# Transposes and mask product in 32-column tiles, and the two parts of an attend back to back, in a recurrent-memory transformer kernel

## The chip, the cores and the metric

The kernel runs on one core of a Trainium2 chip. The metric is the device time of one execution in microseconds (us), the median over runs. Ratios are the mean time of one kernel's fast runs over that of the other's of the same rounds on the same chip, so they are not quite the ratio of the medians that are quoted beside them. A ratio is given with its 95% interval. Profiles are of single executions, and fast runs of one kernel lie up to 15 us (the kernel before) apart, so a difference of some 15 us between two profiles is not clear by itself.

## The reference

Two branches are mixed by a gate. Branch A is a transformer layer with a recurrent memory: 64 segments of 32 tokens, each with 8 memory rows that the segment before it has written. Branch B is a GEGLU feed-forward layer, which does not depend on A.

```python
def _A_ref(x, mem0, Wq, Wk, Wv, Wo, seg_len):        # Dm = 1024, 32 heads of 128, M = 8, seg_len = 32
    mem = mem0
    for s in range(n_seg):                           # 64 segments, each needs mem of the one before
        h = jnp.concatenate([mem, xs], axis=1)       # 40 rows
        q, k, v = (einsum of h with Wq, Wk, Wv)      # cut
        scores = jnp.where(mask, q @ k.T * scale, -1e9)
        o = softmax(scores) @ v
        o = jnp.einsum('bhte,hed->btd', o, Wo)
        mem = o[:, :M, :].copy()
        outs.append(o[:, M:, :])
g = sigmoid((x * gate_w).sum(-1, keepdims=True))
return g * a + (1 - g) * b                           # b = (gelu(x @ w_gate) * (x @ w_up)) @ w_down
```

## The kernel before

The kernel has three parts: a first one of some 100 us that prepares x and a share of the feed-forward layer, the 64 segments (about 25 us each), and the rest of the feed-forward layer from about 1,700 us on. The change touches the segments alone. The kernel does not keep all weights of the attention (four times 8 MB) in SBUF, the on-chip memory: most of each segment's weights are loaded again, by loads of 512 KB into slots.

In a segment the 32 rows of h are the stationary operand of most matmuls, the one that a weight load puts into the array. They fill 32 columns of the array (128*32 in the profile, where the full form is 128*128), so four matmuls run side by side (in the trace they start 3 to 4 ns apart), each in one quarter of the columns and each writing 32 partitions of PSUM, where results are collected. From there a copy evacuates them to SBUF. Three kinds of work leave this tiling: the transposes of the evacuated q and k and the mask product (stationary operand of 128 columns), and the attend (32 rows).

```python
def trans4(e, t=tok):                                     # about five times per segment
    for j in range(4):
        ins = e.transpose(PBV[TT][:, j * 128:(j + 1) * 128], t[:, j * 128:(j + 1) * 128], ident[:, :])
    return ins

def scores(r, mid=None):
    def f(e):
        e.matmul(PB[SS][:, 0:320]..., lhsT=ident[:, :], rhs=mS..., start=True, stop=False)   # the mask, by the array
        for lo, hi, c in ((0, 32, 0), (32, 40, 40)):
            for j in range(4):
                for g in range(4):                        # 32 small matmuls, 32-column tiles
                    ins = e.matmul(PB[SS][32 * g:32 * g + hi - lo, ...], lhsT=qT or qkr, rhs=kT[:, j, g, :], ...)
    ...                                                   # softmax on VectorE and ScalarE: cut

def attend(u):       # 16 matmuls, 32 rows each, into four banks: lhsT=vA[r, j, :], rhs=tA[r, ...]
def attend_tail(u):  # 4 more for the remaining 8 keys: lhsT=vB[r, u, :], rhs=tB[r, ...]; then oT is copied

def proj(p, s):      # one of 64 steps of a segment, 512 KB of weights
    ...              # q, k, v:
                for g in range(4):
                    ins = e.matmul(PB[bk][32 * g:32 * g + 32, :], lhsT=h[:, i, :], rhs=w[:, g * 512:(g + 1) * 512], ...)
    ...              # o:
                for hh in range(2):
                    for g in range(4):
                        c = hh * 1024 + g * 256
                        ins = e.matmul(PB[XO][32 * g:32 * g + 32, 0:256], lhsT=oT[:, gp_, 2 * jj + hh, 0:32], rhs=w[:, c:c + 256], ...)
```

Between the steps stand "fills" (`some(f1, 2)` issues two steps of them), which project the carried rows of later segments. Each segment ends with the carry: the output bank is evacuated, transposed and copied into the next segment's h.

## Time and profile before

| | kernel before |
|---|---|
| median of 3 runs | 2232.4 us (2222.9 to 2234.9) |
| span of the profiled run (an execution of its own) | 2236.0 us |
| 60 segments (third carry to last of 63) | 1479 us, 24.7 us each |
| PE instructions (matmuls and weight loads) | 73,284; 334 more of PE's sequencer |

These are lines of the page of the kernel before. "PE" counts matmuls and "PEld" weight loads; in the 40-slice rows a digit is a tenth; q8 is the queue that brings instructions: packets, MB, share of the engines' time.

```profile
PE 2082.7 (93%) x36642; PEld 1097.3 (49%) x36642; DVE 905.4 (40%) x2152; ACT 611.3 (27%) x1296; POOL 616.0 (28%) x1139
...
PEclk9989999999999999999999999999999999999999
DMA  9977887788788778878887788788779410000000
...
q8 instruction: 287, 4.70, 0.8%
```

PE is busy nearly all the time, and DMA is at 70 to 80% through the segments. The 287 packets are of 16,384 bytes, and 73,284 / 256 = 286 (with the sequencer's instructions 287.6): one packet for 256 PE instructions. Such 256 instructions are called a block here, and the step from one to the next a boundary.

PE's list of waits in the kernel before (line, waited for: us in total, times, longest us). L770 is the output projection, L758 the projections, L992 the carry transposes, L800 a fill.

```profile
PE pb L770 <- issue: 40.2, 38, 2.4
PE pb L992 <- ACT a_bf L658: 12.9, 34, 0.4
PE pb L758 <- issue: 10.0, 10, 1.7
PE pb L758 <- DMA sl<-in_A_Wv_dram: 7.1, 11, 0.9
PE pb L770 <- DMA sl<-in_A_Wo_dram: 5.9, 9, 1.1
PE pb L800 <- issue: 5.3, 8, 1.3
```

"issue" means that PE waited for nothing the profile can name. In the start times of the PE instructions of the segments, counted through with the sequencer's, 54 gaps of over 0.7 us stand at one and the same position of every 256, and no other position has more than two. At each of them the next block's packet had started 2.2 to 2.6 us earlier in nearly every case. So these are waits for instructions. Each of the 70 issue waits of the segments ends within 0.25 us of a boundary, of which there are 247. In the segments the packet of a block starts from 0.7 us before to 5.5 us after the first instruction of the block before it runs, 2.5 us after it in the median.

The timeline of PE in a segment of the kernel before, where two visits to the full tiling can be seen (start, duration, line, tile as rows*columns, count):

```profile
911.88 1.91 PE L758 MATMUL pb<-sl,hT 128*32 128x512 bf16 x32
913.72 0.40 PE L670 MATMUL pb<-ident,tok 128*128 128x128 bf16 x4
914.05 0.83 PE L758 MATMUL pb<-sl,hT 128*32 128x512 bf16 x12
914.81 0.31 PE L685 MATMUL pb<-mS,ident 128*128 128x320 bf16 x1
915.05 0.28 PE L691 MATMUL pb<-kT,qT 128*32 128x40 bf16 x16
```

The start of the first transpose to the start of the next projection is 914.05 - 913.72 = 0.33 us, and the first transpose itself starts 312 ns after the last projection, where a projection would have started after 216 ns. This extra time at a change of tiling, on the way in and on the way out, is called a drain below; the name is no more than that, as the trace does not show what the array does in it. By differences of start times it is 96 to 106 ns on the way in (312 less the 216 or 206 ns from one group of projection matmuls to the next) and 93 to 105 ns on the way out (from the last transpose to a projection 149 ns, less the 56 ns from transpose to transpose; from the mask to the scores 240 ns, less 135).

### The profile page before, as it was taken

To read this page: it belongs to the slowest core of one execution; us is meant where nothing else is said; L and a number is where in the kernel's file an instruction comes from. 1 tells how busy PE (TensorE), PEld (TensorE's weight loads), DVE (VectorE), ACT (ScalarE), POOL (GpSimd) and SP (SyncE) were. 2 spreads that over 40 slices of the span, in tenths; PEclk is the share of its full clock that TensorE was granted. 3 is DMA by queue.
4 is the path that set the end of the run, shared out by engine and by line. 5 is a ranking of instruction groups with operands and counts; after the bars stand their busy time and mean duration, and the time that the engine had idled before them with its cause. 6 is when DMAs were issued, how large, how long until landed. Compare 5 with 4: busy or idle time off the path is not lost.

```text
span 2236.0 us, 80061 instructions
## 1 busy us (share of the span) xinstructions
PE 2082.7 (93%) x36642; PEld 1097.3 (49%) x36642; DVE 905.4 (40%) x2152; ACT 611.3 (27%) x1296; POOL 616.0 (28%) x1139
## 2 busy tenths in 40 slices
PE   7889999999899899999999899999888999999999
PEld 4334555455555555555554555555444444444444
DVE  5433343343344333433443344334334516354362
ACT  4322232223232232322223232223222303122130
POOL 5133334332433343233333323343321000000000
PEclk9989999999999999999999999999999999999999
DMA  9977887788788778878887788788779410000000
GB/s 319 406 274 278 296 305 266 277 309 285 265 303 307 262 266 297 295 280 283 287 293 276 267 304 294 270 284 316 277 268 356 179 38 29 29 24 33 19 29 19
DMA packets 203440, 529.04 MB, mean 237 GB/s; under 512 B 29592, under 2 KB 46616, under 8 KB 203104
## 3 DMA queue, kind: packets, MB, share of 16 engines
q1 hardware_dynamic: 174064, 471.93, 58.9%
q0 software_dynamic: 28896, 51.75, 7.3%
q8 instruction: 287, 4.70, 0.8%
q10 hardware_dynamic: 144, 0.26, 0.1%
q14 instruction: 49, 0.40, 0.0%
HBM read 490.16 MB, written 33.55 MB: 234 GB/s over the span
## 4 chain that ended last, share of the span: by engine, by line
PE 77%; DMA 11%; issue 4%; POOL 4%; DVE 1%; ACT 1%; SPq 1%; DVEq 0%; POOLq 0%; ACTq 0%
PE pb L758 25%; PE pb L446 15%; PE pb L770 9%; PE pb L1098 8%; PE pb L785 7%; PE pb L670 4%; DMA sl<-in_A_Wo_dram 3%; PE pb L800 3%; DMA sl<-in_A_Wv_dram 3%; DMA a_scr<-a_bf 2%; PE pb L691 2%; PE pb L685 1%; POOL v_scr L826 1%; PE pb L1080 1%; PE pb L724 1%
## 5 line engine op out<-in xcount | busy, mean ns | idle before, releaser
L758 PE MATMUL pb<-sl,hT 128*32 128x512 bf16 x12288 | 749.5, 382 | 24.7 <-issue 10.0
L758 PEld LDWEIGHTS pb<-sl,hT 128*32 128x32 bf16 x12288 | 331.2, 97 | 292.1 <-issue 19.9
L770 PE MATMUL pb<-sl,oT 128*32 128x256 bf16 x8192 | 283.1, 276 | 48.9 <-issue 40.2
L658 ACT ACTIVATE tok<-pb 128x512 bf16<-128x512 f32 x317 | 189.3, 597 | 408.6 <-PE pb L758 368.3
L743 POOL COPY oRc<-oT 128x128 bf16<-128x128 bf16 x128 | 96.8, 757 | 645.9 <-DVE oT L661 627.5
L770 PEld LDWEIGHTS pb<-sl,oT 128*32 128x32 bf16 x8192 | 207.7, 97 | 100.8 <-issue 52.9
L785 PE MATMUL pb<-sl,hR 128*32 128x512 bf16 x3072 | 226.6, 385 | 11.3 <-DMA sl<-in_A_Wq_dram 5.1
L446 PE MATMUL pb<-xT,wg 128*128 128x512 bf16 x768 | 182.6, 381 | 2.9 <-DMA wg<-in_B_w_gate_dram 2.9
L446 PE MATMUL pb<-xT,wu 128*128 128x512 bf16 x768 | 182.0, 380 | 0.0
L1098 PE MATMUL pb<-wd,GT 128*128 128x512 bf16 x784 | 169.9, 379 | 0.0
L661 DVE CAST oT<-pb 128x160 bf16<-128x160 f32 x256 | 71.2, 320 | 211.0 <-PE pb L734 210.7
L658 ACT ACTIVATE vA<-pb 128x512 bf16<-128x512 f32 x128 | 76.4, 597 | 267.2 <-PE pb L758 267.2
L434 ACT ACTIVATE s<-pb 128x512 f32<-128x512 f32 x112 | 66.9, 597 | 295.1 <-PE pb L446 295.1
L661 DVE COPY kT<-pb 128x512 bf16<-128x512 bf16 x128 | 51.9, 406 | 228.0 <-PE pb L670 93.7
L670 PE MATMUL pb<-ident,tok 128*128 128x128 bf16 x1268 | 126.7, 222 | 5.5 <-DVE kT L661 2.2
L670 PEld LDWEIGHTS pb<-ident,tok 128*128 128x128 bf16 x1268 | 72.2, 98 | 113.7 <-ACT tok L658 86.0
L435 DVE SCALAR_TENSOR_TENSOR tp<-s,pb 128x512 f32<-128x512 f32 x112 | 76.8, 686 | 125.6 <-ACT s L434 125.3
L1098 PEld LDWEIGHTS pb<-wd,GT 128*128 128x128 bf16 x784 | 76.7, 98 | 92.5
L446 PEld LDWEIGHTS pb<-xT,wg 128*128 128x128 bf16 x768 | 75.2, 98 | 94.2 <-issue 4.6
L696 DVE TENSOR_REDUCE st<-pb 128x8 f32<-128x320 f32 x128 | 63.0, 492 | 142.7 <-PE pb L691 142.6
L446 PEld LDWEIGHTS pb<-xT,wu 128*128 128x128 bf16 x768 | 75.4, 98 | 91.3 <-issue 1.3
L1045 POOL DMA_DIRECT2D out_dram<-osb x14 | 7.6, 545 | 372.5 <-PE pb L446 224.6
(96 smaller groups left out, 2149.3 us busy)
## 6 DMA issues: line engine op xcount, KB each, us to landing
sl<-in_A_Wv_dram SPq DMA_DIRECT2D x394, 512.0 KB, 8.9
sl<-in_A_Wo_dram SPq DMA_DIRECT2D x205, 512.0 KB, 6.1
sl<-in_A_Wk_dram SPq DMA_DIRECT2D x142, 512.0 KB, 5.5
sl<-in_A_Wq_dram SPq DMA_DIRECT2D x79, 512.0 KB, 7.0
qkr<-qk_scr POOLq DMA_DIRECT2D x126, 64.0 KB, 2.2
qk_scr<-stg POOLq DMA_DIRECT2D x61, 128.0 KB, 6.0
wd<-in_B_w_down_dram SPq DMA_DIRECT2D x7, 1024.0 KB, 14.7
px<-in_A_x_dram SPq DMA_DIRECT2D x16, 256.0 KB, 6.7
```

What stands on the lines that cost most here:

```text
L434: op("act", lambda e: e.activation(s1[:, :], hg, ACTF.Square, scale=SQ), rd=[BK(bg)], wr=[s1.r()])
L435: op("dve", lambda e: e.scalar_tensor_tensor(out=t[:, :], in0=s1[:, :], scalar=1.0, in1=hg, op0=ALU.add, op1=ALU.mult), rd=[BK(bg), s1.r() ...
L446: ins = e.matmul(PB[bk][:, 0:FB], lhsT=w[:, kc, cc:cc + 128], rhs=x[:, :, :, kc, :].rearrange("p t i c -> p (t i) c"), start=(kc == 0), st ...
L658: op("act", lambda e: e.activation(o, i, ACTF.Copy), rd=rd, wr=wr)
L661: op("dve", lambda e: e.tensor_copy(o, i), rd=rd, wr=wr)
L670: ins = e.transpose(PBV[TT][:, j * 128:(j + 1) * 128], t[:, j * 128:(j + 1) * 128], ident[:, :])
L743: op("pool", lambda e: e.tensor_copy(oRc[:, u, :, :].rearrange("p c x -> p x c"), oT[:, :, :, 32:40].rearrange("p g j c -> p (g j) c")), r ...
L758: ins = e.matmul(PB[bk][32 * g:32 * g + 32, :], lhsT=h[:, i, :], rhs=w[:, g * 512:(g + 1) * 512], start=(p % 8 == 0), stop=(p % 8 == 7))
L770: ins = e.matmul(PB[XO][32 * g:32 * g + 32, 0:256], lhsT=oT[:, gp_, 2 * jj + hh, 0:32], rhs=w[:, c:c + 256], start=(r == 0 and p % 8 == 0 ...
L785: ins = e.matmul(PB[b][32 * g:32 * g + 32, :], lhsT=h[:, k[2], :], rhs=w[:, g * 512:(g + 1) * 512], start=(n == 0), stop=(n == 7))
L800: ins = e.matmul(PB[b][32 * g:32 * g + 32, 0:256], lhsT=t[:, :, 2 * i + hh], rhs=w[:, c:c + 256], start=(ends[0] and i == 0 and hh == 0), ...
L1098: ins = e.matmul(PB[bank[2 * k + hf]][:, :], lhsT=GT[:, j, tb * 128:(tb + 1) * 128], rhs=w[:, jj, hf * 512:(hf + 1) * 512], start=(j == 0) ...
```

## The change

The intent is to leave the array in the tiling of the projections. Each 128-column transpose and each mask product becomes four 32-column ones, so there is no change of tiling around them. The attend, which must change the tiling, is moved next to its tail, so that both share one visit; the fill steps that stood between them now come first.

```diff
--- before.py
+++ after.py
@@ -667,7 +667,9 @@
 
         def trans4(e, t=tok):
             for j in range(4):
-                ins = e.transpose(PBV[TT][:, j * 128:(j + 1) * 128], t[:, j * 128:(j + 1) * 128], ident[:, :])
+                for g in range(4):
+                    q = slice(32 * g, 32 * g + 32)
+                    ins = e.transpose(PBV[TT][q, j * 128:(j + 1) * 128], t[:, j * 128 + q.start:j * 128 + q.stop], ident[:, :])
             return ins
 
         def trans(to):
@@ -682,8 +684,10 @@
         def scores(r, mid=None):
 
             def f(e):
-                e.matmul(PB[SS][:, 0:320].rearrange("p (a c) -> p a c", a=4), lhsT=ident[:, :],
-                         rhs=mS[:, :].unsqueeze(1).to_broadcast([128, 4, 80]), start=True, stop=False, skip_group_check=True)
+                for g in range(4):
+                    q = slice(32 * g, 32 * g + 32)
+                    e.matmul(PB[SS][q, 0:320].rearrange("p (a c) -> p a c", a=4), lhsT=ident[:, q],
+                             rhs=mS[:, :].unsqueeze(1).to_broadcast([128, 4, 80]), start=True, stop=False, skip_group_check=True)
                 for lo, hi, c in ((0, 32, 0), (32, 40, 40)):
                     for j in range(4):
                         for g in range(4):
@@ -931,9 +935,8 @@
                    rd=[BK(F1), part.r()], wr=[stage[0].r(0, 256)])
 
             on("o", 0, 0, lambda: evac(bank_of["q", 1], tok))
-            on("o", 0, 0, some(f1, 2))
+            on("o", 0, 0, some(f1, 4))
             on("o", 0, 0, lambda: attend(ua))
-            on("o", 0, 0, some(f1, 2))
             on("o", 0, 0, lambda: attend_tail(ua))
             on("o", 0, 0, some(f1, 1))
             on("o", 0, 0, lambda: trans(qT))
@@ -950,9 +953,8 @@
             if uw == 0:
                 on("o", 0, 6, lambda: store_tail(Q, stage[0]))
             on("o", 1, 0, lambda: evac(bank_of["v", 1], vA))
-            on("o", 1, 0, some(f2, 4))
+            on("o", 1, 0, some(f2, 6))
             on("o", 1, 0, lambda: attend(ub))
-            on("o", 1, 0, some(f2, 2))
             on("o", 1, 0, lambda: attend_tail(ub))
             on("o", 1, 0, some(f2))
             if s % 4 == 0 and Q >= 0:
@@ -989,8 +991,12 @@
                 fill_trans()
             if not last:
                 for t, bk in enumerate((B1, B2)):
-                    op("pe", lambda e, t=t, bk=bk: e.transpose(PBV[bk][:, 0:128], a_bf[:, 128 * t:128 * t + 128], ident[:, :]),
-                       rd=[a_bf.r(128 * t, 128 * t + 128), ident.r()], wr=[BK(bk)])
+                    def f(e, t=t, bk=bk):
+                        for g in range(4):
+                            x = 128 * t + 32 * g
+                            ins = e.transpose(PBV[bk][32 * g:32 * g + 32, 0:128], a_bf[:, x:x + 32], ident[:, :])
+                        return ins
+                    op("pe", f, rd=[a_bf.r(128 * t, 128 * t + 128), ident.r()], wr=[BK(bk)])
                     op("dve", lambda e, t=t, bk=bk, h=h_next: e.tensor_copy(
                         h[:, :, NR:32].rearrange("p (g t) c -> p t g c", t=2)[:, t],
                         PBV[bk][:, 0:128].rearrange("p (g c) -> p g c", g=4)[:, :, NR:32]),
```

## The prediction

> **What bounds the kernel.** The page shows PE busy for 93% of the 2236 us span and on 77% of the chain that ended last; DMA is 78% busy until about 1700 us. The 64 recurrent segments take about 25.2 us each (timeline), and the change touches only them. In the list of waits PE waits about 23 us for weight slots and 13 us before the carry transposes; the most, about 60 us, is "issue". In the start times of PE instructions (weight loads and matmuls counted together) nearly all these gaps fall at every 256th instruction. The instruction queue (287 packets of 16 KB, 73,284 PE instructions / 256 = 286) has exactly one packet for each boundary. A boundary that stalls comes 2.2 to 2.6 us after its packet started. So they are instruction fetches. From one boundary to the readiness of the next block takes 4.8 us in the median (2.7 to 7.9), longer with more weight loads in flight; 256 instructions last 5.8 us in the median. About 70 of some 250 boundaries in the segments stall, 70 to 80 us in all.
>
> **What the change removes.** [...] Start to start, projection to projection is 216 ns, projection to transpose 312, last transpose to projection 149 instead of 56, projection to mask 312, mask to scores 240 against the 135 of its 320 columns. Where tilings match, matmul to transpose costs nothing extra. A visit to another tiling costs about 200 ns.
> - Transposes: 290 visits, about 60 us.
> - Mask: 128 visits, about 26 us.
> - Attend with its tail: about 118 visits saved at 180 ns, 21 us.
> - The two carry transposes wait for ACT and end in a DVE copy: about 0.
>
> Together about 105 us (4.7%) of PE time. Streaming stays the same: four 32-column matmuls start 3 to 4 ns apart, and four groups take 25 ns each in the scores, well under the 56 ns of a 128-column group.
>
> **What it adds.** 12 matmuls and 12 weight loads for each of about 320 groups of transposes, 6 instructions for each of 128 masks, 12 for each of 63 carries: about 9,200 PE instructions, 13% more, so 36 more fetches; 256 instructions then last about 4.75 us instead of 5.8, no longer more than the 4.8 us that a fetch needs. Setting the measured fetch times, shuffled, against the block lengths gives 69 us of stalls for the kernel before (measured 70 to 80) and about 190 us after (150 if fetches become 0.3 us quicker, 75 if 1 us). So 80 to 120 us of the gain should return as instruction stalls.
>
> **Prediction.** 2236 us, from 2185 to 2275 8 times in 10. Faster by over 2%: 0.17; within 2%: 0.73; slower by over 2%: 0.10.
>
> **What would show it.** Projection to transpose near 216 ns and transposes to projection near 56; mask to scores near 135; attend to tail about 20 ns. About 82,500 PE matmuls and weight loads together, and about 36 more instruction packets. "Issue" waits up from about 60 us to 130 to 200, at block boundaries and now spread over lines. The second phase (after 1700 us) is unchanged. DMA waits about as before.
>
> **What would make it wrong.** If fetches get quicker because stalls let the weight queue drain, much of the 105 us stays: 2150 to 2190. If the extra 16 KB packets slow each other or the weights, it is over 2275. If a column-tiled transpose does not run four abreast, transposes cost three times more, about 200 us.

What is cut, where marked, was no term of the sum: about 105 us of drains go and 80 to 120 us of stalls come, which leaves about the 2236 us of the profiled run. Three of its statements with their figures from the trace of the kernel before. The 135 ns of the mask's 320 columns is an estimate from the 216 ns of 512 columns. Matmul to transpose "where tilings match" is L446 to L485 in the first part of the kernel: 216 ns at 6 of 11 places, as from one such matmul to the next, and longer at the other five. "Longer with more weight loads in flight": from boundary to packet it is 1.1 us in the median of the 70 boundaries with up to two weight loads in flight and 2.9 of the 177 with three or more (counted afterwards).

## The result

The changed kernel takes 2335.6 us in the median of 4 runs (2329.4 to 2341.6) against 2227.7 us of the kernel before (4 runs): ratio 1.0485 [1.0435, 1.0535], slower by 4.85%. The prediction was 2236 us, so it was wrong.

The same lines of the page, for the changed kernel:

```profile
PE 2035.9 (87%) x41225; PEld 1180.2 (50%) x41244; DVE 906.1 (39%) x2152; ACT 612.0 (26%) x1296; POOL 617.4 (26%) x1139
...
PEclk9989999999999899999999999999999999999999
DMA  9978777777787677777777776787879800001000
...
q8 instruction: 323, 5.29, 0.9%
```

PE is busy for 47 us less, and yet the span is 104 us longer. There are 36 instruction packets more, as predicted.

The timeline of the same stretch of a segment of the changed kernel (L762 projections, L672 transposes, L689 mask, L695 scores):

```profile
933.92 1.90 PE L762 MATMUL pb<-sl,hT 128*32 128x512 bf16 x32
935.72 0.41 PE L672 MATMUL pb<-ident,tok 128*32 128x128 bf16 x16
935.94 0.83 PE L762 MATMUL pb<-sl,hT 128*32 128x512 bf16 x12
936.66 0.32 PE L689 MATMUL pb<-mS,ident 128*32 128x320 bf16 x4
936.80 0.27 PE L695 MATMUL pb<-kT,qT 128*32 128x40 bf16 x16
```

The array does what the change wanted: transposes to projection 935.94 - 935.72 = 0.22 us instead of 0.33, mask to scores 0.14 us instead of 0.24. In the start times, the medians of the entry from a projection (206 ns) and of the exit to one (46 ns) show no drain: a whole visit, from the last projection before the transposes to the first after them, takes 429 ns in the median instead of 639. The drains are gone and the tiled forms run four abreast: four transposes start 4 ns apart in the median, four mask products 3.

PE's list of waits in the changed kernel (L774 output projection, L695 scores, L804 a fill, L997 carry):

```profile
PE pb L774 <- issue: 87.9, 41, 3.8
PE pb L695 <- issue: 41.6, 16, 3.9
PE pb L762 <- issue: 19.5, 22, 2.0
PE pb L672 <- issue: 19.1, 12, 3.1
PE pb L804 <- issue: 19.0, 12, 3.0
PE pb L997 <- ACT a_bf L658: 17.3, 62, 0.4
...
PE pb L762 <- DMA sl<-in_A_Wv_dram: 5.1, 6, 1.7
...
PE pb L774 <- DMA sl<-in_A_Wo_dram: 3.6, 5, 1.3
```

The waits for instructions have tripled and the longest has gone from 2.4 to 3.9 us; all 110 of them in the segments stand at boundaries, of which there are now 280. Waits for weights have not grown.

What follows such a wait is the part that I had not foreseen. The timeline of the changed kernel around one of them:

```profile
945.18 0.74 PE L774 MATMUL pb<-sl,oT 128*32 128x256 bf16 x20
949.56 0.74 PE L774 MATMUL pb<-sl,oT 128*32 128x256 bf16 x20 [3.63 <-issue]
950.11 0.61 PE L672 MATMUL pb<-ident,tok 128*32 128x128 bf16 x16
950.50 1.08 PE L774 MATMUL pb<-sl,oT 128*32 128x256 bf16 x16
951.35 3.00 PE L762 MATMUL pb<-sl,hT 128*32 128x512 bf16 x32
```

Windows of the same stretch (columns: window, length, then busy time and count of PE, PEld, DVE, ACT and POOL, then the granted TensorE clock, the DMA share and GB/s):

```profile
945.00:949.00 4.00, 0.93 (x56) 0.64 (x48) 2.87 (x8) 0.87 (x2) 0.27 (x2) 1.00 1.01 385
950.10:953.50 3.40, 3.40 (x63) 1.90 (x59) 0.00 (x0) 0.60 (x1) 0.78 (x1) 0.51 0.59 205
953.60:957.00 3.40, 3.40 (x92) 1.77 (x88) 0.56 (x2) 1.61 (x4) 0.39 (x1) 1.00 0.05 13
```

Half a microsecond after the end of a wait of 3.63 us, the array runs for 3.4 us at half its clock: the 32 projection matmuls take 3.00 us instead of 1.90. DMA was fully busy while PE waited (1.01 in the first row). The clock records of the changed kernel hold 38 such stretches in its 60 segments, 143 us in all, against 4 and 14 us in the kernel before. In the segments of both traces the records give full clock or half and nothing between, and each record lasts a whole number of 3413 ns. Cut into windows of that length at the ends of the records, the segments show that the window before a stretch was not idle as a whole: the four stretches of the kernel before follow windows in which PE was idle for 0.58 to 0.71, and windows at full clock followed at most 0.59. No threshold is shown: in the changed kernel stretches follow windows idle for as little as 0.47, in z3 (below) for 0.34. Nor does every long wait bring one: of the changed kernel's waits of PE in the segments, 33 of the 44 over 2 us had a stretch that began during them or within 3.4 us after their end, but only 8 of the 71 from 0.5 to 2 us.

A balance of the 60 segments, in us (drains by the prediction's estimate of 105 us for 64 segments, taken for 60; the loss at half clock is the PE time in those stretches less what the same sequence of matmuls takes at full clock on average):

| | before | changed | difference |
|---|---|---|---|
| drains | | | -98 (estimate) |
| idle PE, gaps over 150 ns | 98 | 237 | +139 |
| - of it for instructions ("issue") | 65 | 191 | +126 |
| - of it for ACT and DVE | 22 | 34 | +12 |
| loss at half clock | 6 | 61 | +56 |
| sum of these | | | +97 |
| measured length | 1479 | 1581 | +102 |

### The profile page after: what moved, and what is told of

Same layout as the page of the kernel before. It is cut to its first block, busy times and chain, and to the rows that moved or that the text cites. A ratio compares the mean times of both kernels' runs of the same rounds, so it can differ in the third digit from the quotient of the medians.

```text
span 2339.8 us, 89246 instructions
## 1 busy us (share of the span) xinstructions
PE 2035.9 (87%) x41225; PEld 1180.2 (50%) x41244; DVE 906.1 (39%) x2152; ACT 612.0 (26%) x1296; POOL 617.4 (26%) x1139
## 4 chain that ended last, share of the span: by engine, by line
PE 71%; issue 10%; DMA 9%; POOL 6%; DVE 2%; ACT 1%; SPq 0%; DVEq 0%; POOLq 0%
PE pb L762 22%; PE pb L446 15%; PE pb L774 9%; PE pb L1104 7%; PE pb L789 6%; PE pb L804 3%; PE pb L672 3%; DMA a_scr<-a_bf 2%; POOL v_scr L830 2%; DMA sl<-in_A_Wq_dram 1%; PE pb L695 1%; PE pb L728 1%; PE pb L1086 1%; DMA sl<-in_A_Wv_dram 1%; DMA sl<-in_A_Wo_dram 1%
## 5 line engine op out<-in xcount | busy, mean ns | idle before, releaser
L762 PE MATMUL pb<-sl,hT 128*32 128x512 bf16 x12288 | 776.1, 390 | 36.8 <-issue 19.5
L762 PEld LDWEIGHTS pb<-sl,hT 128*32 128x32 bf16 x12288 | 351.8, 99 | 298.6 <-issue 46.8
L774 PE MATMUL pb<-sl,oT 128*32 128x256 bf16 x8192 | 309.0, 293 | 94.4 <-issue 87.9
L774 PEld LDWEIGHTS pb<-sl,oT 128*32 128x32 bf16 x8192 | 227.1, 103 | 147.1 <-issue 98.7
L789 PE MATMUL pb<-sl,hR 128*32 128x512 bf16 x3072 | 215.3, 387 | 11.8 <-DMA sl<-in_A_Wq_dram 4.8
L446 PE MATMUL pb<-xT,wg 128*128 128x512 bf16 x768 | 183.1, 382 | 5.4 <-DMA wg<-in_B_w_gate_dram 5.4
L446 PE MATMUL pb<-xT,wu 128*128 128x512 bf16 x768 | 181.8, 380 | 0.0
L672 PE MATMUL pb<-ident,tok 128*32 128x128 bf16 x5072 | 136.4, 222 | 28.2 <-issue 19.1
L672 PEld LDWEIGHTS pb<-ident,tok 128*32 128x32 bf16 x5072 | 107.2, 98 | 80.9 <-issue 23.0
L789 PEld LDWEIGHTS pb<-sl,hR 128*32 128x32 bf16 x3072 | 93.0, 98 | 69.1 <-issue 6.7
L446 PEld LDWEIGHTS pb<-xT,wg 128*128 128x128 bf16 x768 | 75.3, 98 | 96.9 <-issue 7.3
L446 PEld LDWEIGHTS pb<-xT,wu 128*128 128x128 bf16 x768 | 75.3, 98 | 91.3 <-issue 1.1
```

Source lines behind the costliest of these rows:

```text
L446: ins = e.matmul(PB[bk][:, 0:FB], lhsT=w[:, kc, cc:cc + 128], rhs=x[:, :, :, kc, :].rearrange("p t i c -> p (t i) c"), start=(kc == 0), st ...
L672: ins = e.transpose(PBV[TT][q, j * 128:(j + 1) * 128], t[:, j * 128 + q.start:j * 128 + q.stop], ident[:, :])
L789: ins = e.matmul(PB[b][32 * g:32 * g + 32, :], lhsT=h[:, k[2], :], rhs=w[:, g * 512:(g + 1) * 512], start=(n == 0), stop=(n == 7))
```

## The experiments

Theory A: the drains are really saved, but the segments are paced by instruction fetches that queue behind the weight loads. More PE instructions, in less time, mean longer waits at block boundaries, and the long ones cost a stretch at half clock on top. Rival B: the tiled forms cost by themselves, in their weight loads or by a lower clock. Rival C: the moved attend delays what depends on it.

All 17 runs gave a result that passed the comparison with the reference. "Segments" is the length of 60 segments in us, "idle" and "half clock" as in the balance, with the number of instruction waits over 1.8 us. These three columns come from the profiled run, of which there is one for each kernel. PE instructions from z1 on are those that the trace recorded, some 20 fewer than issued in places. The ratio of each run is to the kernel before in its own rounds.

| run | PE instructions | median us | ratio to before | segments | idle (issue; over 1.8 us) | half clock: loss |
|---|---|---|---|---|---|---|
| before | 73,284 | 2227.7 | 1 | 1479 | 98 (65; 5) | 6 |
| the change | 82,488 | 2335.6 | 1.0485 [1.0435, 1.0535] | 1581 | 237 (191; 48) | 61 |
| x1 attend alone | 73,284 | 2217.9 | 0.9973 [0.9941, 1.0005] | 1458 | 104 (71; 10) | 1 |
| x2 mask alone | 74,052 | 2232.3 | 1.0051 [1.0003, 1.0099] | 1479 | 116 (82; 14) | 11 |
| x3 transposes alone | 80,964 | 2306.5 | 1.0381 [1.0339, 1.0423] | 1557 | 199 (157; 35) | 33 |
| x4 instructions alone | 80,964 | 2314.9 | 1.0409 [1.0371, 1.0448] | 1554 | 138 (114; 18) | 20 |
| x5 before, no reloads | 73,284 | 2108.6 | 0.9465 [0.9437, 0.9492] | 1369 | 22 (0; 0) | 0 |
| x6 change, no reloads | 82,488 | 2024.8 | 0.9089 [0.9067, 0.9111] | 1290 | 40 (7; 0) | 0 |
| x7 change, 3 loads in flight | 82,488 | 2404.2 | 1.0804 [1.0764, 1.0843] | 1624 | 272 (134; 32) | 58 |
| x8 before, 3 loads in flight | 73,284 | 2388.1 | 1.0737 [1.0669, 1.0804] | 1619 | 182 (13; 2) | 57 |
| y1 no instruction added | 73,284 | 2238.0 | 1.0048 [1.0025, 1.0072] | 1483 | 132 (88; 18) | 16 |
| y2 smaller descriptors | 73,284 | 2271.7 | 1.0203 [1.0173, 1.0233] | 1511 | 117 (73; 9) | 17 |
| y3 change without carry | 81,732 | 2341.5 | 1.0502 [1.0473, 1.0531] | 1569 | 230 (192; 49) | 56 |
| z1 fewer instructions | 65,325 | 2234.4 | 1.0022 [0.9985, 1.0059] | 1469 | 75 (17; 0) | 3 |
| z2 = z1 + attend | 65,325 | 2235.6 | 1.0015 [0.9961, 1.0068] | 1484 | 91 (30; 0) | 20 |
| z4 = z2 + mask | 66,093 | 2224.3 | 0.9994 [0.9952, 1.0037] | 1461 | 100 (36; 4) | 8 |
| z3 = z1 + change but carry | 73,773 | 2296.0 | 1.0295 [1.0255, 1.0336] | 1528 | 181 (131; 29) | 41 |
| z5 = z1, other carry | 65,325 | 2244.0 | 1.0082 [1.0049, 1.0116] | 1476 | 110 (20; 0) | 10 |
| z6 = z4, other carry | 66,093 | 2242.8 | 1.0063 [1.0033, 1.0093] | 1492 | 148 (42; 6) | 25 |

### The parts alone: x1, x2, x3, y3

x1 takes from the change only the new order of attend and fills, x2 only the tiled mask, x3 only the tiled transposes of `tok`; y3 is the changed kernel with the carry transposes in their old form. Their edits are the hunks of the diff above.

> Kernel before with only the attend and its tail put back to back: about 118 drains of 180 ns fewer, no instruction added. Theory A (stalls at the fetch of every 256th PE instruction, each long one followed by a stretch at half clock): 21 us of PE time go, about 7 us of stalls and 2 us of half clock come back, so about 12 us faster, 2216 us, no more long stalls than before (5 over 1.8 us, 4 half-clock windows in the segments). Rival C (the later attend delays the oT copies and the output projection): 10 to 60 us slower, with new waits of the output projection on the oT copies.

> Kernel before with only the mask product in four 32-column tiles: 26 us of drains go, 768 PE instructions come. Theory A: 20 us of stalls and some 7 us of half clock come back, within 10 us of the kernel before, 2228 us. Rival B (matmuls in the new form are slow by themselves): slower in proportion to their share of the change, which is small here, with mask to scores well over 140 ns.

> Kernel before with only the transposes of tok in 32-column tiles: 61 us of drains go, 7,608 PE instructions come. Theory A: stalls rise by about 85 us and half clock by about 30 us, net about 50 us slower, 2280 us, with 30 to 40 stalls over 1.8 us. Rival C: faster by about 50 us, since nothing of the attend moves. Rival B: slower with the time in the transposes themselves (a visit far over 224 ns).

> Changed kernel with the two carry transposes in full form again: 756 PE instructions fewer, drains that mostly hide behind the wait for the evacuation. Theory A: 10 to 20 us faster than the changed kernel, about 2320 us. Rival (the four small pieces save something there): slower than the changed kernel, about 2345 us.

x1 and x2 are within a per cent of the kernel before. In the profile of x1 idle time went up by 6 us, the loss at half clock down by some 5 and the segments are 21 us shorter, about its drains; but that profile is of x1's fastest run, the ratio means 6 us only, and its interval touches 1: a gain is not shown. Rival C wanted 10 to 60 us of loss; for the attend moved alone that is ruled out. x3 alone is 3.8% slower, and its transposes take no longer than planned: the mean of one is 221 ns, as the 222 ns of the old form (lines of the two pages below, before and x3), and a visit takes 429 ns in the median instead of 639. So most of the loss lies with the transposes, although a visit to them is shorter. The expectation for x3 was 50 us and the measurement 84 us by ratio; the stalls rose by 92 us (85 expected) and the loss at half clock by 27. y3 missed: without the tiled carry the change is no faster (1.0502 against 1.0485, in other rounds), so the carry decides nothing.

```profile
L670 PE MATMUL pb<-ident,tok 128*128 128x128 bf16 x1268 | 126.7, 222 | 5.5 <-DVE kT L661 2.2
...
L672 PE MATMUL pb<-ident,tok 128*32 128x128 bf16 x5072 | 134.9, 221 | 20.3 <-issue 9.9
```

### The number of instructions alone: x4

Everything in the old form, with the drains, and ahead of each group of transposes 12 one-column matmuls whose result nobody reads:

```diff
         def trans4(e, t=tok):
+            for n in range(12):
+                q = slice(32 * (n % 4), 32 * (n % 4) + 32)
+                e.matmul(PB[TT][q, 480:481], lhsT=ident[:, q], rhs=ident[:, 0:1], start=True, stop=True, skip_group_check=True)
             for j in range(4):
```

> Kernel before, all in its own form, with 12 one-column matmuls (24 PE instructions with their weight loads) into unused columns ahead of every group of four transposes: as many instructions as the tiled transposes add, no drain taken away, no tiled transpose. Theory A: 20 us of work, 50 us of stalls and 15 us of half clock come: about 85 us slower, 2313 us, and long stalls up from 5 to 20 or more. Rival B or C (the form or the order of the matmuls costs, not their number): only the 20 us of work, 2248 us, long stalls as before.

It is 4.1% slower: 2314.9 us where A said 2313 and its rivals 2248. PE's waits in x4 (L773 output projection, L694 scores, L803 a fill):

```profile
PE pb L773 <- issue: 56.8, 48, 2.5
PE pb L694 <- issue: 23.0, 17, 2.6
...
PE pb L803 <- issue: 11.4, 11, 2.3
```

This is the pattern of the changed kernel without its tiling. Idle time is up by 40 us, the loss at half clock by 14, and the matmuls' own work by some 20 us (an estimate: three groups of four, about 20 ns apart, 320 times): 74 us, and the segments are 75 us longer. Rival B is not needed.

### Without the weight loads: x5 and x6

Each slot is loaded once and never again. The attention then uses wrong weights. The comparison with the reference does not notice, so it says little about the attention branch with these inputs; for z1 to z6, which alter its arithmetic, I compared the output with that of the kernel before in a simulation off the chip, with the attention weights enlarged (difference 0.4% in root mean square; the changed kernel and y1 agree exactly).

```diff
         def fetch(n):
+            if done[n] > 0:
+                return
```

> Kernel before with each weight slot loaded once and never again (wrong result on purpose): DMA nearly idle in the segments. Theory A: a fetch then needs about 2.4 us plus under 1 us, less than 256 instructions last, so the 65 us of issue waits and the 12 us of DMA waits in the segments go: about 80 us faster, 2150 us. Rival (gaps at every 256th instruction do not depend on the weight loads): only the DMA waits go, 2215 us.

> Changed kernel with each weight slot loaded once (wrong result on purpose). Theory A: no stalls and no half clock remain, so the drains are all that differs from the kernel before without loads: about 100 us faster than it, 2050 us. Rival B (the new forms or a lower clock cost by themselves) and C (order of the attend): slower than the kernel before without loads, or equal to it, 2150 to 2250 us, with half-clock windows left.

Now the change wins: 2024.8 us against 2108.6, 4% faster. Lines of the pages of x5 (the first two) and x6, to be read against those of the kernel before and the changed kernel above:

```profile
PE 2037.6 (97%) x36623; PEld 1090.7 (52%) x36642; DVE 904.4 (43%) x2152; ACT 610.3 (29%) x1296; POOL 616.4 (29%) x1139
...
DMA  9931111111111111111111111111058000000000
...
PE 1936.6 (96%) x41225; PEld 1134.0 (56%) x41244; DVE 903.8 (45%) x2152; ACT 610.6 (30%) x1296; POOL 616.3 (30%) x1139
...
PEclk9999999999999999999999999999999999999999
DMA  9941111111111111111111111111085001000000
...
q8 instruction: 323, 5.29, 1.1%
```

The same 323 packets come, but DMA is nearly idle, the issue waits fall from 191 to 7 us and no stretch at half clock is left. From a block boundary to the start of the next block's packet takes 0.3 us in the median in x5 and 0.7 in x6, against 2.5 before and 2.4 in the changed kernel. The segments of x6 are 79 us shorter than those of x5, with 17 us more idle time, so the drains are worth about 79 + 17 = 96 us; 98 had been estimated. This settles that the drains were sized right and that the loss needs the weight loads. x5 gained 110 us where 80 was expected; 82 us of that are the gaps over 150 ns and the half clock, and the other 28 us are in shorter gaps, which I did not follow further.

### Fewer loads in flight, smaller descriptors: x7, x8, y2

```diff
-            op("sp", lambda e: e.dma_start(dst(t, k), src(k)), wr=[t.r()], lane=lane)
+            o = op("sp", lambda e: e.dma_start(dst(t, k), src(k)), wr=[t.r()], lane=lane, after=flight[-3:][:1] if len(flight) >= 3 else ())
+            flight.append(o)
```

> Changed kernel, but a weight load is issued only when the third before it has landed, so at most three are in flight. Theory A: fetch packets wait for less in front of them (in the kernel before 1.2 to 1.8 us with two or three loads in flight, 2.2 to 3.0 with four or five), fetches 0.6 us quicker, stalls down from 191 to about 115 us and most long ones gone: 2240 us or less, 100 us faster than the changed kernel, if the weights still come in time; new waits for weights under 40 us. Rivals B and C: 2335 us or slower.

> Kernel before with at most three weight loads in flight. Theory A: stalls down from 65 to about 35 us, waits for weights up by 10 to 30 us: 2200 to 2235 us. Rival (fetches do not depend on weight loads): slower by the new waits for weights alone, 2240 to 2260 us.

Both times missed by far: the weights come too late. PE's waits in x8 (L760 projections, L772 output projection):

```profile
PE pb L760 <- DMA sl<-in_A_Wv_dram: 135.5, 95, 2.9
PE pb L772 <- DMA sl<-in_A_Wo_dram: 22.2, 31, 1.7
...
PE pb L772 <- issue: 5.8, 9, 2.1
PE pb L760 <- issue: 5.7, 5, 2.3
```

As a remedy this fails, but x8 shows two things. With fewer loads in flight the packet starts 1.7 us after the boundary in the median instead of 2.5, and the issue waits in the segments fall from 65 to 13 us. (The blocks also last longer there, waits for weights included: 6.3 us in the median instead of 5.7. How much of the fall is due to that was not separated.) And the half clock comes back, 143 us of it in the segments, in a kernel with the old forms and hardly any instruction waits: it follows idle time of another cause too, here of weights (182 us idle, 13 of it for instructions). In x7 the packets were no quicker (2.3 us against 2.4 in the changed kernel); why the limit did not help there is open.

y2 splits each q, k and v load into two with rows of 2 KB:

```diff
+            # cut: loads for o stay whole
+            for x in (0, 1024):
+                op("sp", lambda e, x=x: e.dma_start(t[:, x:x + 1024], src(k)[:, x:x + 1024]), wr=[t.r(x, x + 1024)], lane=lane + ("" if x == 0 else "b"))
```

> Kernel before with every q, k and v weight load cut into two loads of 2 KB rows instead of one of 4 KB rows: the same bytes, twice the descriptors. If a fetch packet waits for a number of descriptors in front of it, the median time from block boundary to packet falls from 2.5 us and stalls fall to 30 to 50 us: 2190 to 2210 us. If it waits for bytes, the stalls stay at 60 to 70 us, and the time is that of the kernel before or longer by what smaller descriptors cost the weights, 2225 to 2260 us.

The packets wait as long as before (2.4 us in the median), so what a packet waits for is not a fixed number of descriptors ahead of it. In the segments of the kernel before, a 2,048-byte packet of the queue of the loads takes 96 ns in the mean and one of 4,096 bytes 179, so the same bytes in halves take 7% longer; y2 is 2% slower.

### Drains without added instructions: y1

x1, and the mask product in its old form issued directly after the transposes of qT, so that both share a visit. The order of the attend's four banks changes with it (second line).

```diff
+            on("v", 0, 5, lambda: (trans(qT), mask()))     # instead of trans(qT), and no mask in scores; the same in "o", 0, 0
+        bo = (B0, SS, B1, B2)     # instead of (B0, B1, B2, SS); other lines cut
```

> A version meant to beat both: attend and tail back to back, and the mask product in its old full form moved to stand directly after the transposes of qT, so that both share one visit to the full tiling. 47 us of drains go and not one instruction is added. Theory A: 10 to 15 us come back as stalls of shorter blocks, so 2195 us, 1 to 1.5% faster than the kernel before, with at most 15 long stalls. Rival (removing drains is worth nothing here because stalls take all of it back): 2220 to 2230 us.

A miss for my own theory as I had sized it: not faster by 1%, but 0.5% slower. The transpose-to-mask step is 56 ns as planned, so some 44 us of drains are gone (estimate: the expected 47 us, taken for 60 segments), but idle time rose by 34 us (instructions 65 to 88, weights 12 to 21) and the loss at half clock by 10. Block fetches and weight loads take the gain back even where nothing is added. Why it did worse than x1, which leaves the mask and the banks as they were, is open.

### Fewer instructions: z1 to z6

z1 does the output projection with four matmuls of 512 columns a step instead of eight of 256. Column groups 0 and 1 take one head, groups 2 and 3 the other; the two partial sums are added by the carry's matmul (a selection matrix as moving operand) and, for the store, by VectorE.

```diff
-                    for hh in range(2):
-                        for g in range(4):
-                            c = hh * 1024 + g * 256
-                            ins = e.matmul(PB[XO][32 * g:32 * g + 32, 0:256], lhsT=oT[:, gp_, 2 * jj + hh, 0:32],
-                                           rhs=w[:, c:c + 256], ...)
+                    for g in range(4):
+                        ins = e.matmul(PB[XO][32 * g:32 * g + 32, :], lhsT=oT[:, gp_, 2 * jj + g // 2, 0:32],
+                                       rhs=w[:, g * 512:(g + 1) * 512], ...)
     # cut: carry by  e.matmul(PB[bk][:, 16 * cc:16 * cc + 16], lhsT=a_bf[:, 128 * c:128 * c + 128], rhs=Rr), four of them
```

> Kernel before with the output projection in four matmuls of 512 columns a step instead of eight of 256: each column group takes one head and one half of the outputs, the two partial sums are added when the carry is transposed (by a selection matrix as moving operand) and, for the store, by VectorE. 8,192 PE instructions fewer (11%), some 12 us more of streaming, no drain taken away. Theory A: stalls fall from 65 to about 25 us, long ones nearly all gone: about 40 us faster than the kernel before, 2188 us. Rival (the count of instructions is not what matters): 2235 to 2245 us, slower by the streaming.

> z1 with attend and tail back to back (no instruction added, 21 us of drains go). Theory A: 15 us faster than z1, 2172 us, as stalls no longer take the gain back. If drains are worth nothing whatever the stalls are: the time of z1.

> z2 with the mask product in four 32-column tiles (768 PE instructions, 26 us of drains). Theory A: 10 us faster than z2, 2162 us. If the weight loads set the pace by now: the time of z2, with waits for weights in place of stalls.

> The whole change except the carry, on the output projection of z1: about as many PE instructions as the kernel before (73,540 against 73,284) and 105 us of drains fewer. Theory A: 2195 us, faster than the kernel before but no faster than z1 to z4, stalls of about 115 us with 20 long ones. If the tiled transposes cost beyond their instruction count: slower than the kernel before.

The stalls did as A said: issue waits in the segments 65 to 17 us in z1, none over 1.8 us. The time did not: 1.0022 [0.9985, 1.0059]. The carry has become longer (768 ns from the last output projection to its first matmul instead of 657, and about 800 ns over its four pieces instead of 168 over two), and waits for weights are 26 us instead of 12. The 12 us more of streaming that were expected are not shown: two groups of 256 columns, 109 ns each in the kernel before, became one of 512 columns, about 215 ns in z1. z2 and z4 gain nothing clear over z1, with weight waits of 38 and 37 us. z3 bears most directly on the question: the change without the carry at nearly the instruction count of the kernel before is still 2.95% slower, with 131 us of issue waits. So the total count is not what decides, but the time that a block's work takes. Blocks without their stall last 5.2 us in the median in z3 and 5.7 in the kernel before, and a fetch takes no less than before (5.2 us in the median against 4.9, taken as the time from boundary to packet plus the 2.4 us from packet to readiness). Over the runs the issue waits go with the share of blocks whose work is shorter than 4.9 us: 5% in z1 (17 us of waits), 22% in the kernel before (65), 31% in x4 (114), 34% in z3 (131), 36% in x3 (157), 46% in the changed kernel (191).

z5 and z6 replace the four evacuations before the carry by two of 256 columns, on ScalarE and VectorE at once:

```diff
-            for c, eng in ((0, "act"), (2, "dve"), (1, "act"), (3, "act")):
+            for c, eng in ((0, "act"), (1, "dve")):
```

> z1 with the evacuation before the carry in two copies of 256 columns, one on ScalarE and one on VectorE at the same time, instead of four of 128 of which three queue on ScalarE. Theory A: about 0.3 us less per segment than z1, 20 us: 2212 us, 0.8% faster than the kernel before, stalls about 20 us. Rival (weights set the pace whatever PE does): the time of z1, 2234 us, with waits for weights up by 15 to 20 us.

> z4 (attend and tail back to back, mask in four tiles, fewer instructions in the output projection) with the same shorter carry. Theory A: 2200 us, 1.2% faster than the kernel before and 0.5% faster than z5. Rival (weights set the pace): no faster than z5, waits for weights above 45 us.

Both are slower than the kernel before, by less than 1%. The carry did not get shorter, but longer: now PE waits for both copies (L999 carry, L764 the first projection of the next segment, in z5):

```profile
PE pb L999 <- ACT a_bf L664: 21.5, 63, 0.6
PE pb L999 <- DVE a_bf L667: 17.3, 63, 0.3
...
PE pb L764 <- DVE hT L1003: 14.7, 63, 0.2
```

So whether a good carry would let z1's fewer instructions pay was not tested. No version with its weight loads beats the kernel before beyond its interval; x1 comes nearest.

## Why the prediction was wrong

- **Drains: right.** About 200 ns a visit and 105 us in all was predicted; x6 against x5 gives 96 us in 60 segments, and the spacings are those that were listed as signs (46 to 56 ns at the exit, 135 ns from mask to scores).
- **More and tighter fetches: right in kind, a little small.** "So 80 to 120 us of the gain should return as instruction stalls": 126 us came. "Issue" waits of 130 to 200 us were predicted and 198 us are in the list. The fetch times stayed what they had been (2.5 and 2.4 us in the median from boundary to packet), so taking the measured ones was fair. Pairing them at random with block lengths was less so: redone with the blocks of the changed kernel's trace, it gives about 152 us of stalls, not 191. x4 and x5 with x6 show the cause by experiment, from both sides.
- **The step that failed** is the sum itself: stalls were entered at their own length and nothing else. The runs showed that most of the changed kernel's waits over 2 us (33 of 44) are followed by 3.4 us at half clock. In the kernel before, 5 waits were over 1.8 us and 4 stretches at half clock cost 6 us, so the term did not show. The same shuffling, redone from the traces, gives about 29 waits over 1.8 us with the changed kernel's blocks (measured 48) and 8 with those of the kernel before, so the term could have been priced. The loss was 61 us, 56 more than before. New waits for ScalarE and VectorE, which the sum did not have either, added 12 us. Without the half clock the segments would have grown by about 46 us (102 - 56, an estimate), so it is the largest term left out, but not the whole miss.
- **The predicted sum** was -105 us of drains and 80 to 120 us of stalls, about 0; with the drains as estimated for 60 segments and the other terms as measured it is -98 + 126 + 12 + 56 = 96 of the 102 us by which the segments grew. About 6 us are not placed.
- **The ways to be wrong** that I had listed did not happen: fetches neither got quicker nor slower, and tiled transposes do run four abreast. The right way was not on the list.
- **Not settled:** y1, and why x7's limit did not quicken the fetches. That stalls and half clock depend on weight loads is shown by x5, x6 and x8; what exactly a fetch packet queues behind is only inferred. y2 speaks against a fixed number of descriptors.

## What to carry to other kernels

Where PE issues many short matmuls while DMA is busy, count PE instructions per microsecond and compare the time of 256 of them with the time of a fetch under load (here 4.9 us in the median for 5.7 us of work, and about 5 us of work after the change): splitting an instruction into four to save a drain can cost more in fetches than the drain (x3: about 61 us of drains by estimate against 92 us more of stalls). Look at gaps with the releaser "issue", and see whether they come every 256 instructions. And price a long idle time of PE twice, once as idle and once as the stretch at half clock that may stand behind it (in the changed kernel behind 33 of the 44 waits over 2 us).
